# Seven 64x64 block products for eight in the first MLP product of 24 tiles

## The chip, the cores and the metric

The kernel runs on one core of one Trainium2 chip. The metric is the time of one execution on the device, in microseconds (us). Times inside the profile count from the first instruction of one profiled execution; its span ends with the last instruction.

## What is computed

The reference is polysketched attention followed by an MLP with an exact gelu. Cut to what matters (4 batches, 4 heads, 1088 tokens of 32 channels; 4352 tokens of 128 channels in the MLP, 2048 hidden channels):

```python
phi = lambda x: outer(S1 @ x, S2 @ x)          # 8 x 8 = 64 features per token and head
kv, z = sum_s phi(k) v, sum_s phi(k)           # per batch and head
x = (phi(q) @ kv) / (phi(q) @ z + 1e-6)        # -> (4352, 128)
h = x @ w_in                                   # (4352, 2048): the first MLP product
g = 0.5 * h * (1 + erf(h / sqrt(2)))
out = g @ w_out                                # (4352, 128): the second MLP product
```

All of it is in float32.

## The kernel before, in words

**Chunks, tiles, steps.** The tokens are worked in nine chunks n. Chunks 0 to 7 have 512 tokens (two for each batch), chunk 8 has 256, the remainders of all batches. `NMAIN` is 8, `NCH` 2, `NF` 16, `NB` 4. A hidden tile (n, fi) is 128 of the 2048 hidden channels for the tokens of a chunk; four tiles form a block (n, b), stored in one of three `block` buffers. The main loop (L1163) goes over the list `steps` of tiles. The first sixteen steps alternate between chunks 0 and 1; from step 32 on, step t is tile t % 16 of chunk t // 16. So step 64 opens chunk 4 and step 96 chunk 6; step 128 opens chunk 8.

**One step.** `hidden(n, fi)` (L715) multiplies a 128x128 piece of `w_in` with `xT[n]` (128 channels x 512 tokens) into one of two PSUM banks called `h_ps`, as two matmuls of 64 output rows that share the array, and then issues gelu on ACT into the block (L728). After that come `token_sums` if the block is complete, what stands in `slots[t]`, stores in `done[t]` and second products in `products[t]`; drains in `drains[t]` come ahead of the tile. A matmul in the text is two MATMUL instructions in the profile.

**The second product** already uses seven block products for eight. `token_sums` (L764) makes four sums of gelu outputs on POOL (L772 to L775), `channel_sums` has made sums of `w_out`, and `two_products` (L794) multiplies two 128x64 blocks of 256 tokens at a time (L807) into the two `o_ps` banks `acc[n]`. A block has seven such pairs. `drain(n)` (L812) adds the banks up on ACT and DVE into the `sums` tiles, and `store(n)` (L860) finishes with `combine` (L841, L842), a transpose on DVE (L869) and DMAs from SP.

**Where x comes from.** `query_sketch` (L578), `attend_products` (L633) and, for keys, `features_of_all` (L977) use small tiles of the array. `take_x(n)` (L638) copies the attention result of a chunk from `w_ps` banks to `xT[n]` on ACT (L644). For chunks 6, 7 and 8 all this is done in `last_attends` at step 95; chunks 6 and 7 share two `w_ps` banks there.

**Rounding and key work.** At steps 4 to 14 the weights arrive. Key and query transposes (L368, L528) and `query_outer` run on DVE at steps set by `at(t, ...)`.

**What sets the order.** All of it is written out by hand: the lists above give each piece a step, and at the end of the function every instruction is tied to the one before it on its engine, so that each engine works in the order of the text:

```python
    for ins in nc.cur_bb.bb.instructions:
        if ins.engine in last:
            tc.add_manual_dep(ins, last[ins.engine].name, ...)
        last[ins.engine] = ins
```

PSUM has eight banks: two `h_ps`, two `o_ps`, and two `w_ps` tiles of two banks each. A tile's buffer is given on when all that read it are done.

Of the kernel before, what the change touches and what calls it, by code (L numbers as in the profile page):

```python
# [8 lines left out]
FP = mybir.dt.float32  # L9
U32 = mybir.dt.uint32  # L10
AX = mybir.AluOpType
ACT = mybir.ActivationFunctionType
# [4 lines left out]
def kernel(  # L17
# [18 lines left out]
    pe, dve, act, pool, sp = nc.tensor, nc.vector, nc.scalar, nc.gpsimd, nc.sync  # L36
# [5 lines left out]
    NF = d_ff // 128  # L42
# [24 lines left out]
    def work_banks():  # L67

        return wps.tile([128, 2, CW], FP, name="w_ps")
# [645 lines left out]
    def hidden(n, fi, by_halves=False):  # L715
        W = width[n]
        ps = first_banks.pop((n, fi)) if (n, fi) in first_banks else hidden_bank()
        w = w_tile(w_in_sb, fi)
        for rows in (slice(0, 64), slice(64, 128)) if by_halves else (slice(0, 128),):
            if (n, fi) not in begun:  # L720
                pe.matmul(ps[rows, :W], lhsT=w[:, rows], rhs=xT[n][:, :W], start=True, stop=True)  # L721
# [6 lines left out]
        act.activation(out=g_of[n, fi][:, :W], in_=ps[:, :W], func=ACT.Gelu)  # L728
# [61 lines left out]

    def first_block(n):
        return USUAL // NB if n < NCH else 0

    def two_products(n, b, i):  # L794
# [8 lines left out]
        for name, e in zip(two[:2], two[2:]):  # L803
# [3 lines left out]
            pe.matmul(acc[n][bank][half * 64:(half + 1) * 64, col:col + HW], lhsT=fixed, rhs=moving,  # L807
                      start=opens and e == 0 and name in "4715", stop=b == NF // NB - 1, skip_group_check=True)

    drained = {}  # L810

    def drain(n):  # L812


        C, N = (att.tile([128, 2, CW], FP, name="sums") for i in range(2))
        lo, hi, one, two = slice(0, 64), slice(64, 128), slice(0, HW), slice(HW, CW)
        a0, a1 = acc[n]

        act.copy(out=C[lo, 0], in_=a1[hi])
        act.copy(out=N[hi, 0, one], in_=C[lo, 0, one])  # L820

        dve.tensor_copy(out=N[lo, 0, one], in_=a0[lo, one])  # L822
# [4 lines left out]
        dve.tensor_add(out=C[hi, 0, two], in0=a0[hi, two], in1=C[hi, 0, one])  # L827
        dve.tensor_add(out=N[hi, 1, one], in0=a0[hi, one], in1=C[hi, 0, two])
        drained[n] = C, N
# [137 lines left out]
    def at(t, f, *a):  # L967
        slots[t].append(lambda: f(*a))
# [64 lines left out]
    def last_attends():  # L1033

        banks = work_banks()
        attend_products(NMAIN - 2, banks)
        attend_products(NMAIN - 1, banks[:, :, CW // 2:])
        attend_products(NMAIN)
        for n in range(NMAIN - 2, NCHUNK):
            take_x(n)  # L1040

    def turn_keys_rem(pair):
        held["rem"] = work_bank()
# [86 lines left out]
                at(t + 10, turn_first_kv)  # L1130


    products = {t: [] for t in range(len(steps) + LAG)}
    done = {t: [] for t in range(len(steps) + LAG + 1)}
    drains = {t: [] for t in range(len(steps) + LAG + 1)}
    for t, (n, fi) in enumerate(steps):
        if n < NCH and fi < USUAL:
            products[t + LAG].append((project, n, fi))
            if fi == USUAL - 1:
                slots[t + LAG + 1 + 2 * n].append(lambda n=n: take_usual(n))  # L1140
        elif n == NMAIN:
            at_ = max(t + LAG, (n * NF + 5) if fi < 3 else (n * NF + 6) if fi < 5 else 0)
            if fi < NF - 4:
                products[at_].append((project, n, fi))
            if fi == NF - 1:

                products[at_] += [(project, n, NF - f, (i,)) for f, i in ((4, 0), (3, 0), (2, 0), (4, 1), (1, 0), (3, 1),
                                                                          (2, 1), (1, 1))]
                done[at_ + 1].append(n)
        elif fi % NB == NB - 1:  # L1150
            b = fi // NB
            opens = b == first_block(n)
            late = int(n < NCH or n == NCH and opens)
            for later, pairs in ((3, 3), (4, 2), (5, 2)) if opens else ((2, 2), (3, 2), (4, 1), (5, 2)):
                later += late
                for i in range(pairs):
                    products[t + later].append((two_products, n, b, len([p for q in products.values() for p in q
                                                                        if p[:3] == (two_products, n, b)])))
            if b == NF // NB - 1:
                drains[t + 6 + late].append(n)  # L1160
                done[t + 12].append(n)

    for t in range(len(steps) + LAG):  # L1163
        if t < 4:

            hidden(0, t)
            if t == 1:
                w_out[0].low_words()
                w_out[0].exponents()
                w_out[0].finish()  # L1170
                w_out[1].fields()
            if t == 2:
                w_out[1].low_words()
            if t == 3:
                banks = work_banks()
                numerators_by_token(1, halves(banks), range(JC))
                w_out[1].mantissas(by_pool=True)
                w_out[1].exponents()
                divide(1, banks, range(JC), by_head_pair=False)
                w_out[1].signs()  # L1180
                w_out[1].product()
                project(0, 0)
                project(0, 1, cols=slice(0, 256))
                turn_half(1, 0, work_bank(), by_act)
                project(0, 1, cols=slice(256, 512))
                turn_half(1, 1, work_bank(), by_dve)
            continue
        if t == 4:
            first_hidden(1, 0)
            for f, *a in products[t]:  # L1190
                f(*a)
            first_hidden(1, 1)
        for n in drains[t]:
            drain(n)
        sooner = t == NMAIN * NF
        if sooner:
            for f, *a in products[t]:
                f(*a)
        if t < len(steps):
            n, fi = steps[t]  # L1200
            hidden(n, fi, by_halves=t >= 18 and (n < NMAIN or fi < 5))
        if t < len(steps) and steps[t][0] < NMAIN and steps[t][1] % NB == NB - 1:
            n, b = steps[t][0], steps[t][1] // NB
            if b >= first_block(n):
                token_sums(n, b)
        for f in slots[t]:
            f()
        for n in done[t]:
            store(n)
        if t != 4 and not sooner:  # L1210
            for f, *a in products[t]:
                f(*a)
# [41 lines left out]
```

## Time and profile before

| | |
|---|---|
| median of 3 timed runs | 259.19 us (259.15 to 259.4) |
| span of the profiled execution (the page gives no other time of it) | 257.9 us |
| busy: PE, DVE, ACT, POOL | 253.1, 151.1, 115.2, 163.6 us |
| mean granted TensorE clock | 0.999 |
| L721 matmuls (first product), 514 instructions | 136.9 us busy |
| L728 gelu of 512 tokens, 112 instructions | 598 ns each |
| L807 matmuls (second product), 128x64 by 256 tokens | 379 ns each |
| L772 to L775, the sums on POOL | 1278 to 1288 ns each |

PE is TensorE's matmuls, DVE VectorE, ACT ScalarE, POOL GpSimd, SP the engine that issues DMAs. Matmuls overlap one another, so the busy time of single instructions is longer than their share of the stream; the chain of waits gives the share. The chain of waits is followed back from the last instruction and is listed with start, length, and engine and line. In timelines a line gives start, length, engine, line and operation, and in brackets how long the engine had been idle and who released it.

### The profile page before, as it was taken

How to read it: one execution, taken by the hardware profiler on the slowest of the kernel's cores; microseconds unless marked ns; L12 is line 12 of the kernel's file. 1: busy time of each engine (PE TensorE's matmuls, PEld its weight loads, DVE VectorE, ACT ScalarE, POOL GpSimd, SP SyncE). 2: the span in 40 equal slices, each digit the busy share in tenths (PEclk: the TensorE clock that was granted, in tenths of full speed). 3: DMA queues.
4: the chain of work that ended last, by engine and by line, in shares of the span. 5: the costliest groups of instructions: out<-in, count | busy, mean ns of one | idle time of the engine just before them, and what ended most of it. 6: DMA issues, size and time to landing. Idle time of an engine off the chain costs nothing.

```text
span 257.9 us, 5770 instructions
## 1 busy us (share of the span) xinstructions
PE 253.1 (98%) x2335; PEld 135.5 (53%) x2335; DVE 151.1 (59%) x313; ACT 115.2 (45%) x224; POOL 163.6 (63%) x173
## 2 busy tenths in 40 slices
PE   8989999999999999999999999999999999999995
PEld 7846444354444545444444455455544444445794
DVE  3786888969699997590178986399307000700330
ACT  4665777433626332543335332533444334433442
POOL 3313006799968778587758775787758777877300
PEclk9999999999999999999999999999999999999999
DMA  6459747751000101102000002000200200020020
GB/s 203 143 156 375 181 117 174 211 131 15 4 0 13 29 3 23 20 8 35 3 0 3 0 10 37 0 1 3 41 3 5 38 0 1 7 36 0 3 41 20
DMA packets 29594, 13.48 MB, mean 52 GB/s; under 512 B 21888, under 2 KB 27776, under 8 KB 29568
## 3 DMA queue, kind: packets, MB, share of 16 engines
q1 hardware_dynamic: 29392, 13.05, 20.2%
q8 instruction: 18, 0.29, 0.5%
q10 hardware_dynamic: 176, 0.07, 0.1%
q14 instruction: 8, 0.07, 0.1%
HBM read 10.88 MB, written 2.23 MB: 51 GB/s over the span
## 4 chain that ended last, share of the span: by engine, by line
PE 93%; SPq 2%; DMA 2%; DVE 1%; issue 0%; ACT 0%
PE h_ps L721 45%; PE o_ps L807 33%; PE o_ps L858 5%; PE w_ps L855 3%; DMA small<-in_moe_w_in_dram 2%; PE w_ps L437 1%; PE w_ps L578 1%; PE w_ps L633 1%; SPq L132 1%; PE h_ps L737 1%; SPq L100 1%; PE w_ps L977 1%; PE w_ps L656 0%; SPq L118 0%; PE w_ps L467 0%
## 5 line engine op out<-in xcount | busy, mean ns | idle before, releaser
L721 PE MATMUL h_ps<-xT,w_in 128*64 128x512 f32 (+3 forms) x514 | 136.9, 576 | 0.0
L728 ACT ACTIVATE block<-h_ps 128x512 f32<-128x512 f32 (+1 forms) x128 | 73.1, 571 | 117.2 <-PE h_ps L721 115.3
L721 PEld LDWEIGHTS h_ps<-xT,w_in 128*64 128x64 f32 (+1 forms) x514 | 41.9, 142 | 30.5 <-issue 11.6
L807 PE MATMUL o_ps<-block,w_out 128*64 128x256 f32 x224 | 57.5, 379 | 0.0
L772 POOL TENSOR_TENSOR bits_low<-block 128x512 f32<-128x512 f32 x28 | 36.0, 1286 | 27.7 <-ACT block L728 27.7
L807 PEld LDWEIGHTS o_ps<-block,w_out 128*64 128x64 f32 x224 | 30.5, 137 | 38.0 <-issue 27.5
L773 POOL TENSOR_TENSOR bits_a<-block 128x512 f32<-128x512 f32 x28 | 35.8, 1278 | 11.8 <-ACT block L728 11.8
L822 DVE COPY sums<-o_ps 64x256 f32<-64x256 f32 x8 | 3.3, 417 | 60.6 <-PE o_ps L807 60.6
L774 POOL TENSOR_TENSOR bits_e<-bits_a,block 128x512 f32<-128x512 f32 x28 | 36.1, 1288 | 2.2
L775 POOL TENSOR_TENSOR bits_m<-block,bits_e 128x512 f32<-128x512 f32 x28 | 35.9, 1282 | 2.2
L807 PE MATMUL o_ps<-bits_a,small 128*64 128x256 f32 x112 | 28.8, 379 | 0.0
L807 PE MATMUL o_ps<-bits_low,small 128*64 128x256 f32 x112 | 28.8, 379 | 0.0
L807 PE MATMUL o_ps<-block,small 128*64 128x256 f32 x112 | 28.8, 379 | 0.0
L807 PE MATMUL o_ps<-bits_m,w_out 128*64 128x256 f32 x112 | 28.7, 379 | 0.0
L807 PEld LDWEIGHTS o_ps<-block,small 128*64 128x64 f32 x112 | 15.2, 137 | 17.9 <-issue 10.8
L807 PE MATMUL o_ps<-bits_e,small 128*64 128x256 f32 x112 | 17.0, 383 | 0.0
L858 PE MATMUL o_ps<-g,w_out 128*128 128x512 f32 (+1 forms) x34 | 16.5, 572 | 0.0
L807 PEld LDWEIGHTS o_ps<-bits_m,w_out 128*64 128x64 f32 x112 | 15.3, 137 | 0.0
L807 PEld LDWEIGHTS o_ps<-bits_a,small 128*64 128x64 f32 x112 | 15.2, 137 | 0.0
L807 PEld LDWEIGHTS o_ps<-bits_low,small 128*64 128x64 f32 x112 | 15.2, 137 | 0.0
L590 DVE STREAM_TRANSPOSE w_ps<-w_ps 128x512 f32<-128x512 f32 (+1 forms) x7 | 4.8, 687 | 17.1 <-ACT xT L644 12.7
L807 PEld LDWEIGHTS o_ps<-bits_e,small 128*64 128x64 f32 x112 | 7.7, 137 | 10.6 <-issue 8.8
(195 smaller groups left out, 303.7 us busy)
## 6 DMA issues: line engine op xcount, KB each, us to landing
block<-in_moe_w_in_dram SPq DMA_DIRECT2D x3, 512.0 KB, 11.3
block<-in_moe_w_out_dram SPq DMA_DIRECT2D x3, 512.0 KB, 14.7
k<-in_k_dram SPq DMA_DIRECT2D x12, 128.0 KB, 2.9
v<-in_v_dram SPq DMA_DIRECT2D x12, 128.0 KB, 3.5
q<-in_q_dram SPq DMA_DIRECT2D x24, 64.0 KB, 2.1
out_dram<-oT SPq DMA_DIRECT2D x21, 64.0 KB, 2.2
k<-in_k_dram SPq DMA_DIRECT2D x2, 256.0 KB, 2.8
q<-in_q_dram SPq DMA_DIRECT2D x2, 256.0 KB, 3.9
```

Of the source, the lines that this page charges most:

```text
L100: eng.dma_start(out=main[n, b][:, heads], in_=src_of[n][b, heads, 0:MAIN, :].rearrange("h (p j) d -> p h j d", j=J))
L590: dve.transpose(out=tok, in_=ps[:, :, :H2])
L721: pe.matmul(ps[rows, :W], lhsT=w[:, rows], rhs=xT[n][:, :W], start=True, stop=True)
L728: act.activation(out=g_of[n, fi][:, :W], in_=ps[:, :W], func=ACT.Gelu)
L772: pool.tensor_sub(out=s[3], in0=a11, in1=a21)
L773: pool.tensor_add(out=s[1], in0=a21, in1=a22)
L774: pool.tensor_sub(out=s[2], in0=s[1], in1=a11)
L775: pool.tensor_sub(out=s[4], in0=a12, in1=s[2])
L807: pe.matmul(acc[n][bank][half * 64:(half + 1) * 64, col:col + HW], lhsT=fixed, rhs=moving, start=opens and e == 0 and name in "4715", stop ...
L822: dve.tensor_copy(out=N[lo, 0, one], in_=a0[lo, one])
L855: pe.matmul(o_of[n][i][:, :128], lhsT=g[:, i * 128:(i + 1) * 128], rhs=w_tile(w_out_sb, fi), start=first, stop=final)
L858: pe.matmul(o_of[n][:, cols], lhsT=w_tile(w_out_sb, fi), rhs=g[:, cols], start=first, stop=final)
```

## The change

For the blocks (6,2), (6,3) and (7,0) to (7,3), which are 24 of the 128 full tiles, the first product is done in 64x64 blocks. For each pair of tiles, the 2x2 split is over the input channels (upper and lower 64 partitions), the hidden channels (the two tiles) and the tokens (two halves of 256); seven block products stand for eight. It needs sums of `w_in` (`weight_sums`, at steps 57 to 61, kept in tiles of old keys and values), sums of x (`x_sums`, in place of `take_x` for chunks 6 and 7), and copies and additions of partial results (`keep`, `add_to`) before the gelus. Products chain up in one PSUM bank per pair (`chain`), whose partial values are copied out on the way, and in a second bank (`side`).

In the same fourteen slots of such a group (`seven_groups`), the second product of the block two earlier is done in halves of 64 rows, each half into banks of its own (`by_rows`); `keep_rows`, `add_rows` and `drain_rows` bring the two halves together. In each slot two 64x64 tiles work on the lower and two on the upper partitions. The groups stand where step 104 was; steps 104 to 127 do nothing else.

```diff
+    def weight_sums(i):
+        ...
+        ps = work_banks()
+        for to, of in ((LO, HI), (HI, LO)):
+            act.copy(out=ps[to, 0, :n], in_=w_in_sb[i][of])
+        w, o = (t.rearrange("p (q f c) -> p q f c", f=2, c=128) for t in (w_in_sb[i], ps[:, 0, :n]))
+        odd, two = (ps[:, 1, x:x + n // 2].rearrange("p (q c) -> p q c", c=128) for x in (0, HW))
+        act.copy(out=odd, in_=w[:, :, 1])
+        s1, s2, s3, s4 = (t[:, at] for t in WS)
+        dve.tensor_add(out=s1, in0=o[:, :, 1], in1=w[:, :, 1])
+        dve.tensor_sub(out=two, in0=s1, in1=o[:, :, 0])
+        dve.tensor_sub(out=s3, in0=w[:, :, 0], in1=odd)
+        dve.tensor_sub(out=s4, in0=w[:, :, 0], in1=two)
+        act.copy(out=s2, in_=two)
+
+    def x_sums(n):
+        ps = numerators_in[n]
+        take_x(n)
+        ...
+        a, b, pa, pb = xT[n][:, :HW], xT[n][:, HW:], ps[:, 0, :HW], ps[:, 1, :HW]
+        for to, of in ((LO, HI), (HI, LO)):
+            act.copy(out=sb[to], in_=pb[of])
+        dve.tensor_sub(out=t1, in0=pb, in1=a)
+        for to, of in ((LO, HI), (HI, LO)):
+            dve.tensor_sub(out=across[to], in0=pb[of], in1=a[of])
+        dve.tensor_sub(out=t2, in0=pb, in1=across)
+        dve.tensor_sub(out=t4, in0=pa, in1=t2)
+        dve.tensor_sub(out=t3, in0=sb, in1=pb)
+
+    PAIR_AT = {"1": 0, "2": 1, "6": 3, "7": 6, "5": 7, "4": 10, "3": 11}
+    OUT_AT = {0: (1, 2, 4, 8, 9, 10, 11), 64: (0, 4, 5, 6, 7, 12, 13)}
+
+    def pair_product(n, b, k, name):
+        rows, p = (LO, HI)[(k + (name in "2346")) % 2], 2 * b + k
+        for e in range(2):
+            w = w_tile(w_in_sb, 2 * p + (name == "4")) if name in "124" else WS["5673".index(name)][:, p]
+            pe.matmul((chain if name in "1674" else side)[k][e * 64:(e + 1) * 64], lhsT=w[rows, e * 64:(e + 1) * 64],
+                      rhs=XS[n][name][rows], start=name in "125", stop=True, skip_group_check=True)
+
+    def keep(k, i, copy):
+        copy(out=part[k][i], in_=chain[k])
+
+    def add_to(k, to, i):
+        dve.tensor_add(out=results[k][:, to], in0=side[k], in1=part[k][i])
+
+    def after_slot(s, n, b):
+        return {0: [(keep, 0, 0, by_dve)], 1: [(add_to, 0, 0, 0)], 2: [(keep, 1, 0, by_act)],
+                3: [(keep, 0, 1, by_act), (add_to, 1, 0, 0)], 5: [(keep, 1, 1, by_dve)], 6: [(keep, 0, 2, by_dve)],
+                7: [(add_to, 0, 1, 2)], 8: [(keep, 1, 2, by_act)], 9: [(add_to, 1, 1, 2), (pair_gelu, n, b, 0, "both")],
+                10: [(pair_gelu, n, b, 0, "chain")], 11: [(add_to, 0, 2, 1), (pair_gelu, n, b, 1, "both")],
+                12: [(pair_gelu, n, b, 1, "chain")],
+                13: [(add_to, 1, 2, 1), (pair_gelu, n, b, 0, "third"), (pair_gelu, n, b, 1, "third"), (token_sums, n, b)]}.get(s, [])
+
+    def seven_groups(groups, outs, extra):
+        ...
+            for s in range(14):
+                for rows in (LO, HI):
+                    if s in OUT_AT[rows.start]:
+                        row_products(m, mb, OUT_AT[rows.start].index(s), rows)
+                    ...  # pair_product of this slot and these rows
+                for f, *a in after_slot(s, n, b) + extra.get((i, s), []):
+                    f(*a)
...
+        if n == NMAIN - 1:
+            for i in (1, 0):
+                add_rows(i, by_rows[0][i])
...
-        for n in range(NMAIN - 2, NCHUNK):
-            take_x(n)
+        for n in range(NMAIN - 2, NMAIN):
+            x_sums(n)
+        take_x(NMAIN)
...
+    for i, t in ((3, 57), (4, 58), (2, 59), (1, 60), (0, 61)):
+        at(t, weight_sums, i)
+    seven = [(n, b) for n in range(NMAIN - 2, NMAIN) for b in range(NF // NB)]
+    extra = {(3, 5): [(keep_rows, 1)], (3, 8): [(add_rows, 1)], (4, 0): [(keep_rows, 0)], (4, 3): [(add_rows, 0)]}
...
-            at_ = max(t + LAG, (n * NF + 5) if fi < 3 else (n * NF + 6) if fi < 5 else 0)
+            at_ = max(t + LAG, n * NF + (9 if fi < 3 else 10 if fi < 6 else 11 if fi < 9 else 0))
...
+            if n == NMAIN - 2:
+                continue
+            if n == NMAIN - 1:
+                ...  # blocks 2 and 3 of chunk 7 by two_products from steps 128 and 133 on; drain at 137, store at 139
...
-                done[t + 12].append(n)
+                done[t + (12 if n < NMAIN - 3 else 7)].append(n)
...
+            if steps[t] == (NMAIN - 2, 2 * NB):
+                seven_groups(seven[2:], seven[:-2], extra)
+                for i in (1, 0):
+                    keep_rows(i)
+                drain_rows(NMAIN - 2)
+                store(NMAIN - 2)
...
-            hidden(n, fi, by_halves=t >= 18 and (n < NMAIN or fi < 5))
+            hidden(n, fi, by_halves=t >= 18 and (n < NMAIN or fi < 9))
```

`row_products` is `two_products` for one half of the rows, `keep_rows` copies a bank of the upper rows to SBUF on ACT, `add_rows` adds it to the lower rows' bank on DVE, and `drain_rows` is `drain` on those sums. `pair_gelu` is the gelu of two quarters ("both") or of one ("third", "chain").

More of the change, by code (lines that the diff above doesn't have):

```diff
@@ L808, in two_products, with row_products @@
                       start=opens and e == 0 and name in "4715", stop=b == NF // NB - 1, skip_group_check=True)
-    drained = {}
+    LO, HI = slice(0, 64), slice(64, 128)
+    by_rows, begun_rows = {}, set()
+    def row_products(n, b, i, rows):
+        names = (("4", "7"), ("4", "7"), ("6a", "6b"), ("1", "5"), ("1", "5"), ("2", "3"), ("2", "3"))[i]
+        es = ((0, 0), (1, 1), (0, 1), (0, 0), (1, 1), (0, 0), (1, 1))[i]
+        for name, e in zip(names, es):
+            half, bank, col = PLACE[name]
+            moving, fixed = factor(n, b, name, e)
+            first = (n, half, bank, rows.start) not in begun_rows
+            begun_rows.add((n, half, bank, rows.start))
+            pe.matmul(by_rows[rows.start][bank][half * 64:(half + 1) * 64, col:col + HW], lhsT=fixed[rows], rhs=moving[rows],
+                      start=first, stop=False, skip_group_check=True)
@@ new lines @@
+    words_of = lambda t: t.rearrange("p h j d -> p (h j d)")
+    WS, XS = [], {}
+    def weight_sums(i):
+        if not WS:
+            WS.extend(words_of(main[x]).rearrange("p (q c) -> p q c", c=128) for x in (("k", 0), ("v", 0), ("k", 1), ("v", 1)))
+        c0, c1 = pieces[i]
+        n, at = c1 - c0, slice(c0 // 256, c1 // 256)
+        ps = work_banks()
[10 more added lines that the diff above has]
+        act.copy(out=s2, in_=two)
@@ new lines, in x_sums @@
+    def x_sums(n):
+        ps = numerators_in[n]
+        take_x(n)
+        t = words_of(main["kv"[n % 2], 3]).rearrange("p (k x) -> p k x", x=HW)
+        sb, t4 = (mlp.tile([128, CW], FP, name="g", bufs=4)[:, :HW] for i in range(2))
+        t1, across, t2, t3 = (t[:, i] for i in range(4))
+        a, b, pa, pb = xT[n][:, :HW], xT[n][:, HW:], ps[:, 0, :HW], ps[:, 1, :HW]
[7 more added lines that the diff above has]
+        dve.tensor_sub(out=t3, in0=sb, in1=pb)
+        XS[n] = {"1": a, "2": a, "3": b, "4": t4, "5": t1, "6": t2, "7": t3}
@@ new lines @@
+    PAIR_AT = {"1": 0, "2": 1, "6": 3, "7": 6, "5": 7, "4": 10, "3": 11}
+    OUT_AT = {0: (1, 2, 4, 8, 9, 10, 11), 64: (0, 4, 5, 6, 7, 12, 13)}
+    chain, side, part, results = {}, {}, {}, {}
+    def pair_product(n, b, k, name):
[4 more added lines that the diff above has]
+                      rhs=XS[n][name][rows], start=name in "125", stop=True, skip_group_check=True)
@@ new lines, in keep, with pair_gelu @@
+    def keep(k, i, copy):
+        copy(out=part[k][i], in_=chain[k])
+    def add_to(k, to, i):
+        dve.tensor_add(out=results[k][:, to], in0=side[k], in1=part[k][i])
+    def pair_gelu(n, b, k, which):
+        to = blocks[n, b][:, 2 * k:2 * k + 2].rearrange("p f (h x) -> p (f h) x", h=2)
+        r = results[k]
+        out, of = {"both": (to[:, 0::3], r[:, 0:2]), "third": (to[:, 1], r[:, 2]), "chain": (to[:, 2], chain[k])}[which]
+        act.activation(out=out, in_=of, func=ACT.Gelu)
@@ new lines, in seven_groups @@
+    def seven_groups(groups, outs, extra):
+        one, two = [hidden_bank(), hidden_bank()], work_banks()
+        by_rows[64] = halves(work_banks())
+        by_rows[0] = [out_bank(), out_bank()]
+        for k in range(2):
+            chain[k], side[k] = one[k][:, :HW], two[:, k, :HW]
+            results[k] = words_of(main["kv"[k], 2]).rearrange("p (k x) -> p k x", x=HW)
+            part[k] = [words_of(q_sb[4 + k])[:, :HW], words_of(q_sb[4 + k])[:, HW:], words_of(q_sb[6])[:, k * HW:(k + 1) * HW]]
+        for i, ((n, b), (m, mb)) in enumerate(zip(groups, outs)):
+            acc[m] = by_rows[0]
+            blocks[n, b] = block(FP)
+            for f in range(NB):
+                g_of[n, b * NB + f] = blocks[n, b][:, f]
+            for s in range(14):
+                for rows in (LO, HI):
+                    if s in OUT_AT[rows.start]:
+                        row_products(m, mb, OUT_AT[rows.start].index(s), rows)
+                    for k in range(2):
+                        for name, t in PAIR_AT.items():
+                            if t + 2 * k == s and (k + (name in "2346")) % 2 == rows.start // 64:
+                                pair_product(n, b, k, name)
+                for f, *a in after_slot(s, n, b) + extra.get((i, s), []):
+                    f(*a)
@@ new lines, with keep_rows, add_rows, drain_rows @@
+    kept, whole = ([words_of(q_sb[x + i]) for i in range(2)] for x in (0, 2))
+    def keep_rows(i):
+        act.copy(out=kept[i], in_=by_rows[64][i])
+    def add_rows(i, to=None):
+        dve.tensor_add(out=whole[i] if to is None else to, in0=by_rows[0][i], in1=kept[i])
+    drained = {}
+    def drain_rows(n):
+        C, N = (att.tile([128, 2, CW], FP, name="sums") for i in range(2))
+        lo, hi, one, two = LO, HI, slice(0, HW), slice(HW, CW)
+        a0, a1 = whole
+        act.copy(out=C[lo, 0], in_=a1[hi])
+        act.copy(out=N[hi, 0, one], in_=a1[hi, one])
+        dve.tensor_add(out=N[lo, 1, one], in0=a0[lo, two], in1=a0[lo, one])
+        dve.tensor_add(out=C[lo, 1], in0=a1[lo], in1=C[lo, 0])
+        for half in (lo, hi):
+            dve.tensor_add(out=C[half, 0, one], in0=a0[lo, one], in1=C[lo, 1, two])
+        dve.tensor_add(out=C[hi, 0, two], in0=a0[hi, two], in1=C[hi, 0, one])
+        dve.tensor_add(out=N[hi, 1, one], in0=a0[hi, one], in1=C[hi, 0, two])
+        drained[n] = C, N
@@ L1151 @@
             b = fi // NB
+            if n == NMAIN - 2:
+                continue
+            if n == NMAIN - 1:
+                for later, pairs in ((0, 2), (1, 2), (2, 1), (3, 2)) if b > 1 else ():
+                    for i in range(pairs):
+                        products[NMAIN * NF + later + 5 * (b == 3)].append((two_products, n, b, len([
+                            p for q in products.values() for p in q if p[:3] == (two_products, n, b)])))
+                if b == NF // NB - 1:
+                    drains[137].append(n)
+                    done[139].append(n)
+                continue
             opens = b == first_block(n)
@@ L1198 @@
                 f(*a)
+        if t < len(steps) and steps[t][0] in (NMAIN - 2, NMAIN - 1) and (steps[t][0], steps[t][1] // NB) in seven[2:]:
+            if steps[t] == (NMAIN - 2, 2 * NB):
[4 more added lines that the diff above has]
+                store(NMAIN - 2)
+            assert not (slots[t] or products[t] or drains[t] or done[t])
+            continue
         if t < len(steps):
             n, fi = steps[t]
-            hidden(n, fi, by_halves=t >= 18 and (n < NMAIN or fi < 5))
+            hidden(n, fi, by_halves=t >= 18 and (n < NMAIN or fi < 9))
         if t < len(steps) and steps[t][0] < NMAIN and steps[t][1] % NB == NB - 1:
```

## The prediction

> **What bounds the kernel now.** I read the page's busy times first, then the chain of waits, then ACT's and DVE's timelines where the change puts work.
>
> ```profile
> PE 253.1 (98%) x2335; PEld 135.5 (53%) x2335; DVE 151.1 (59%) x313; ACT 115.2 (45%) x224; POOL 163.6 (63%) x173
> PEclk9999999999999999999999999999999999999999
> ```
>
> TensorE is busy throughout at full granted clock, so a shorter stream of products shortens the kernel, and anything that makes PE wait lengthens it one for one. The chain of waits around the steps that get new work:
>
> ```profile
> 119.71 0.43 PE o_ps L807 x4
> 120.15 0.86 PE h_ps L721 x4
> 121.00 0.86 PE o_ps L807 x8
> 121.87 0.86 PE h_ps L721 x4
> ...
> 126.17 0.59 PE w_ps L578 x16
> 126.76 0.43 PE w_ps L633 x16
> 127.19 0.43 PE w_ps L977 x16
> 127.62 0.58 PE o_ps L807 x4
> 128.21 0.86 PE h_ps L721 x4
> ```
>
> A hidden tile (L721) takes 0.86 us, a pair of second-product blocks (x4, L807) 0.43, so a usual step is 1.72. From step 32 on, step t is tile t%16 of chunk t//16: 128.21 is step 64, 120.15 step 60, 115.41 step 57, 184.92 step 96. The L578/L633/L977 bursts show eight 64x32 tiles of the array at work together: 16 instructions of 256 columns in 0.43, the time in which two 128x64 tiles do 4.
>
> ```profile
> 103.19 0.60 ACT L728 ACTIVATE block<-h_ps 128x512 f32<-128x512 f32 x1 [1.04 <-PE h_ps L721]
> 103.68 0.26 ACT L468 COPY kz<-w_ps 128x128 f32<-128x128 f32 x1
> ```
>
> ACT works in the order of the text. A 512-wide operation lasts 0.60, but an independent next one starts 0.49 after it; a 256-wide one lasts 0.39 (next after 0.29). ACT's gelu of a tile must end before PE writes the tile two steps later (two h_ps banks).
>
> ```profile
> 193.15 0.42 DVE L822 COPY sums<-o_ps 64x256 f32<-64x256 f32 x1 [10.22 <-PE o_ps L807]
> ...
> 195.41 0.43 DVE L827 TENSOR_TENSOR sums<-o_ps,sums 64x256 f32<-64x256 f32 x1
> 195.88 0.43 DVE L828 TENSOR_TENSOR sums<-o_ps,sums 64x256 f32<-64x256 f32 x1
> 196.34 0.82 DVE L841 TENSOR_TENSOR sums<-sums 64x256 f32<-64x256 f32 x1
> 197.17 0.42 DVE L842 TENSOR_TENSOR sums<-sums 64x256 f32<-64x256 f32 x1
> 197.63 0.71 DVE L869 STREAM_TRANSPOSE oT<-sums 128x512 f32<-128x512 f32 x1
> ```
>
> A DVE operation of 256 columns with a PSUM operand takes 0.41 to 0.43, a dependent one starts 0.46 after it, an independent one about 0.36. DVE is in chunk 5's drain and store until 198.34.
>
> **The seven-product groups: -2.58.** A block of four tiles now costs PE 4 x 0.86 + 7 x 0.43 = 6.45. In a group it is 28 + 28 quarter products (64x64, 256 columns), four at a time: 14 slots of 0.43 = 6.02. Six groups save 6 x 0.43 = 2.58. That a slot takes 0.43 with four tiles is taken from L633 and L977 (eight tiles, 0.43). Entering a 64-row mode costs 0.16 (L578's 0.59 against 0.43), leaving it 0.15 (L807 x4 in 0.58): +0.31, bounds 0.15 and 0.31.
>
> Inside a group the chain bank must be copied out (`keep`) two slots (0.86) before it is written again. Data are readable 0.22 after the product gives way to the next (tile 58's gelu starts at 118.04, the product behind tile 58 at 117.82), the copy takes 0.41, PE restarts 0.10 after a release (xT's copy ends 184.65, the product starts 184.75): 0.73 against 0.86, no stall. By kinder and harsher hand-overs 0 to 0.14 per tight slot, with `add_rows` about 2 in all; I take 0, and keep 2 for the range. ACT has about 3.9 of 6.02 to do (3 copies and 4 gelus of 0.39, 2 gelus of 0.60), DVE nine operations of 0.41 = 3.7, POOL its four sums of 1.28 plus gaps = 5.3: each fits. The Trainium skill, "TensorEngine Tiling (Array Packing)", PSUM Bottleneck, speaks against the change: tiling speeds TensorE but not the emptying of PSUM, which may become the bound. By that rule a group would last as long as its busiest emptier, 3.9 by the rows above, so it would not bind here.
>
> **First group's first copy: +1.9.** Steps 101 to 103 lose their products (moved into the groups), so they run at 0.86 each from 193.10, and the groups begin at 195.7 on the chain. The copy of `chain[0]` after slot 0 stands on DVE behind chunk 5's drain and store (whose end, 198.34, does not move). It would be ready at 196.3, starts at 198.3, ends at 198.7; slot 3, due at about 196.95 by PE's own row, starts at 198.85. Everything behind it on PE waits 1.9. Bounds 1.4 (if L841 takes 0.42) and 2.1.
>
> **weight_sums at steps 57 to 61: +6.0.** For a 512-wide piece, with the step's gelu starting at G, ACT issues copies at G+0.49 and +0.98 (ends +1.56) and `odd` at +1.47. DVE: s1 at +1.61, `two` at +2.07 (ends +2.48), s3 +2.43, s4 +2.84 (ends +3.25). ACT's last copy, s2, reads `two`; the next gelu is queued behind it. Two bounds: s2 starts when `two` is there (+2.53; next gelu +2.82), or, as s3 and s4 read the same PSUM bank and stand ahead in the text, when s4 is done (+3.30; next gelu +3.59). The trace has ACT and DVE on one bank at the same time nowhere that I looked: in the drain DVE's L823 (193.60) starts after ACT's read of that bank (L819, 192.99 to 193.57), while L822, on the other bank, runs beside it. L823 also needs L819's result, so this is no proof; I take the later start, nearest to that row. The Trainium skill, "PSUM — Partial Sum Buffer", PSUM bank collisions raise a hardware error, says that two engines may not touch one bank and quadrant at once, reads included, so that a program must order them; by it W is 6.0, without it 3.7. No run here shows it yet.
>
> With 3.59 for 512-wide pieces and, likewise, 2.65 for the two 256-wide ones (128-wide operations 0.26 to 0.29), gelus start at 116.32 (step 57), 119.91, 123.50, 127.09, 129.74, 132.39 (step 62). PE restarts on the chain 0.27 after a release (184.65 to 184.92). Tile 60, due at 120.15, needs gelu 58 (ends 120.51): 120.78. Tile 61 needs gelu 59: 124.37. Tile 62: 127.96. Tile 63: 130.61. Gelu 63 starts at 132.88, chunk 4's `take_x` runs 133.37 to 133.96, tile 64 starts at 134.23 instead of 128.21: +6.0. Chunk 2's store (1.5 of DVE) and key transposes (1.26) now stand behind these sums and mostly fit. With 2.82 the same walk gives +3.7. Over both readings and quicker or slower hand-overs: 2.2 to 8.5. ACT's copies alone, without the way over DVE, would give 0.
>
> **x_sums at step 95: +1.5.** `take_x(6)` 184.06 to 184.65 stays, so tile 96 starts as now. Behind it on ACT: two 64x256 copies (end 185.23), then `take_x(7)`, which reads the same two banks as chunk 6's six DVE operations. If ordered behind them (185.28 to 187.6), ACT goes on 187.65, 188.14, 188.43, `take_x(8)` 188.72, and tile 96's gelu runs 189.0 to 189.6 instead of from 185.91; tile 98, due 188.37, starts 189.87: +1.5. If banks may be shared, that gelu starts at 186.5 and the cost is 0. The same choice as above; bounds 0 and 1.8. The rest of DVE's work ends before the drain of 193.15, now 1.5 later too.
>
> **After the groups: +0.5.** ACT has the last gelus (about 1.0 past the end), two `keep_rows` and two copies of `drain_rows` before tile 128's gelu, which ends about 3.1 past; tile 130, due at 2.7, starts at 3.2. Bounds 0 and 0.9. Chunk 6's drain and store and chunk 7's later one (5.6 of DVE, 2.6 of SP issue) end before PE does: after chunk 7's last product PE still has 7 x 0.43 + 64 x 0.11 = 10.1. POOL's last sums end 6.4 past the groups, needed at 8.6.
>
> **The other edits, nothing.** The new times of chunk 7's and chunk 8's products and `by_halves` up to tile 8 change the order of PE's work, not its amount; chunk 5's store, five steps earlier in the text, already runs right after its drain (196.34), so DVE and SP see no change; `drain`'s two `add_rows` (0.68 each) lie in the 10.1 that PE still has.
>
> **Sum.** -2.58 + 0.31 + 1.9 + 6.0 + 1.5 + 0.5 = +7.6. The span would go from 257.9 to 265.5. The page gives the profiled execution no time but its span; the timed median, 259.19, lies 1.29 above it, and nothing at either end changes: 266.8 us.
>
> **Rivals.** (a) ACT and DVE may read one bank together: 3.7 for 6.0 and 0 for 1.5, +3.8: 263.0. For it: nothing in the rows forbids it. Against: the drain's order. (b) Faster: ACT's sums fit its idle time. Place: steps 57 to 63 (and 95); ACT has 1.23 idle per step, the copies take 1.56 for three steps and 1.02 for two. If the way over DVE costs ACT nothing, W and x_sums are 0, the sum is +0.1, and with the low ends elsewhere (1.4, 0.15, 0) -1.0: 258.2. It decides from W below 0.5. Against: s2 stands ahead of the next gelu and needs two dependent DVE results. (c) The hand-overs in the groups are too long for two slots: +2 more, 268.8. (d) Four quarter tiles do not run at 0.43: each 0.01 per slot costs 0.84 over 84 slots; at 0.50, 272.7. Against: L633, L977.
>
> **Numbers.** Forecast 0.63, its own range 264.5 to 269; (a) 0.11; (b) 0.12; (c) 0.10; (d) 0.04. The range, 260.3 to 270.5, leaves out most of (b), (d) and the harsh end of weight_sums. A measurement of this kernel can tell about 0.2% (0.5 us) from no change. Faster: most of (b) and no other, 0.09; within 0.2%: the rest of (b) and the kindest end of (a), 0.04; slower 0.87.
>
> **What would show it.** In the chain after: tiles 60 to 64 late by 6 in all, PE idle before L721 released by ACT's gelu; ACT's s2 copies starting after s4. A gap of 1.9 at slot 3 of the first group released by DVE; then slots of 0.43, groups of 6.02. I am wrong if ACT keeps pace in steps 57 to 63 (then near 259), or if a slot is not 0.43.

## The result

The changed kernel takes **286.03 us** (median of 4 runs, 285.02 to 286.83); the kernel before, run beside it, 259.26 (4 runs, 259.15 to 259.4). The ratio is 1.1027 (95% interval 1.0999 to 1.1056): 26.8 us slower, where +7.6 was forecast and the range ended at 270.5. The profiled execution took 285.02 us with a span of 283.2, which is 25.3 above the span before; the steps below are laid against that. The times measured for the runs below are medians, and a run over 1.5% longer than the fastest of its kernel is left out (there is one, 277.52 us, of `e4_sides_apart`).

The busy times and the clock row of the changed kernel's page:

```profile
PE 265.0 (94%) x2751; PEld 143.3 (51%) x2751; DVE 191.8 (68%) x402; ACT 134.3 (47%) x282; POOL 164.0 (58%) x173
PEclk9999999999999999989999999999988999999999
```

PE was busy 98% of a span of 257.9 and is now busy 94% of one of 283.2. The clock row, flat in the kernel before, has two dips, each at or just behind a place where PE waited for over 2 us.

The chain of waits of the changed kernel at steps 57 to 64 (start, length, engine and line):

```profile
114.99 0.88 PE h_ps L721 x4
115.90 0.60 ACT block L728
116.52 0.59 ACT w_ps L836
117.14 0.59 ACT w_ps L836
117.75 0.39 ACT w_ps L839
118.16 0.44 DVE k L841
118.62 0.44 DVE w_ps L842
...
119.42 0.42 DVE v L844
119.87 0.37 ACT v L845
120.24 0.50 ACT block L728
...
136.48 1.08 PE h_ps L721 x4
```

Before, this stretch of the chain was PE alone. Now it goes through ACT (L836 the two copies, L839 `odd`, L845 s2) and DVE (L841 to L844, s1, `two`, s3, s4), and returns to a gelu (L728); in ACT's timeline the first four of these gelus start at 115.90, 120.14, 124.46 and 128.70, 4.24 to 4.32 us apart. Step 57's tile starts at 114.99 (before: 115.41) and step 64's at 136.48 (before: 128.21): `weight_sums` costs 0.42 + 8.27 = 8.7.

The first group, DVE's timeline of the changed kernel (start, length, engine, line, operation, idle time before and its releaser):

```profile
206.55 0.43 DVE L968 TENSOR_TENSOR sums<-o_ps,sums 64x256 f32<-64x256 f32 x1
206.99 0.83 DVE L981 TENSOR_TENSOR sums<-sums 64x256 f32<-64x256 f32 x1
207.83 1.39 DVE L982 TENSOR_TENSOR sums<-sums 64x256 f32<-64x256 f32 x1
209.26 0.71 DVE L1009 STREAM_TRANSPOSE oT<-sums 128x512 f32<-128x512 f32 x1
210.00 0.42 DVE L878 COPY q<-h_ps 128x256 f32<-128x256 f32 x1
210.53 0.42 DVE L881 TENSOR_TENSOR k<-w_ps,q 128x256 f32<-128x256 f32 x1
```

The group begins on PE at 206.37; its first copy (`keep`, L878) and first addition (`add_to`, L881) stand behind chunk 5's drain and store. That is as forecast, except that PE waits for the addition too, as its timeline has it:

```profile
211.01 0.69 PE L874 MATMUL w_ps<-xT,w_in 64*64 64x256 f32 x2 [3.12 <-DVE k L881]
```

The group lasts to 218.40, 12.03 instead of 7.9.

A later group, DVE's timeline and then PE's (only its products into `w_ps`, the tile of the two `side` banks; two rows are the four MATMULs of one side product):

```profile
231.96 0.42 DVE L881 TENSOR_TENSOR v<-w_ps,q 128x256 f32<-128x256 f32 x1 [0.82 <-ACT block L888]
233.13 0.42 DVE L881 TENSOR_TENSOR k<-w_ps,q 128x256 f32<-128x256 f32 x1 [0.75 <-PE h_ps L874]
234.31 0.42 DVE L881 TENSOR_TENSOR v<-w_ps,q 128x256 f32<-128x256 f32 x1 [0.75 <-PE w_ps L822]
...
235.49 0.42 DVE L881 TENSOR_TENSOR k<-w_ps,q 128x256 f32<-128x256 f32 x1 [0.25 <-PE w_ps L874]
```

```profile
232.44 0.43 PE L874 MATMUL w_ps<-xT,v 64*64 64x256 f32 x2 [0.15 <-DVE v L881]
232.71 0.38 PE L874 MATMUL w_ps<-xT,v 64*64 64x256 f32 x2
233.62 0.43 PE L874 MATMUL w_ps<-xT,v 64*64 64x256 f32 x2
233.88 0.38 PE L874 MATMUL w_ps<-xT,v 64*64 64x256 f32 x2
234.79 0.43 PE L874 MATMUL w_ps<-xT,w_in 64*64 64x256 f32 x2
...
235.97 0.43 PE L874 MATMUL w_ps<-xT,w_in 64*64 64x256 f32 x2
```

The two pairs' side products alternate, k into one bank, v into the other. Each begins 0.06 or 0.07 after the addition that reads the *other* bank has ended (232.38, 233.55, 234.73, 235.91): 1.17 or 1.18 from one to the next, where two slots are 0.86. PE's row at 232.44 names an addition on DVE as what released it.

At step 95, in `x_sums`, the chain runs from chunk 6's last DVE operation (L862) over `take_x(7)` (L644) to tile 96's gelu and tile 98:

```profile
196.16 0.34 DVE k L862
...
196.52 0.05 ACT xT L644
...
198.28 0.49 ACT block L728
...
198.82 1.08 PE h_ps L721 x4
```

POOL's first sum of each group gives the period (its timeline, L772 alone):

```profile
219.57 1.27 POOL L772 TENSOR_TENSOR bits_low<-block 128x512 f32<-128x512 f32 x1 [7.87 <-ACT block L888]
227.42 1.27 POOL L772 TENSOR_TENSOR bits_low<-block 128x512 f32<-128x512 f32 x1 [2.65 <-ACT block L888]
235.27 1.27 POOL L772 TENSOR_TENSOR bits_low<-block 128x512 f32<-128x512 f32 x1 [2.64 <-ACT block L888]
243.60 1.27 POOL L772 TENSOR_TENSOR bits_low<-block 128x512 f32<-128x512 f32 x1 [3.12 <-ACT block L888]
251.79 1.27 POOL L772 TENSOR_TENSOR bits_low<-block 128x512 f32<-128x512 f32 x1 [2.99 <-ACT block L888]
259.64 1.28 POOL L772 TENSOR_TENSOR bits_low<-block 128x512 f32<-128x512 f32 x1 [2.63 <-ACT block L888]
```

Five periods of 7.85, 7.85, 8.33, 8.19 and 7.85, together 40.07; the same work took 5 x 6.45 = 32.25 before, and 5 x 6.02 = 30.1 was forecast.

All the steps of the span: -0.42 up to step 57, +8.7 `weight_sums`, +0.2 to step 95, +1.95 `x_sums`, +0.4 to the groups, +5.6 the first group (12.03 - 6.45), +7.8 the other five, +1.1 after them (24.6 from the groups' end instead of 23.5). Sum: +25.3.

### The profile page after: what moved, and what is told of

Its sections match the earlier page's. It is cut to its first block, busy times and chain, and to the rows that moved or that the text cites. A ratio compares the mean times of both kernels' runs of the same rounds, so it can differ in the third digit from the quotient of the medians.

```text
span 283.2 us, 6810 instructions
## 1 busy us (share of the span) xinstructions
PE 265.0 (94%) x2751; PEld 143.3 (51%) x2751; DVE 191.8 (68%) x402; ACT 134.3 (47%) x282; POOL 164.0 (58%) x173
## 4 chain that ended last, share of the span: by engine, by line
PE 76%; DVE 9%; ACT 7%; POOL 4%; issue 2%; DVEq 0%; POOLq 0%; ACTq 0%
PE h_ps L721 31%; PE o_ps L807 21%; PE o_ps L998 5%; PE w_ps L874 4%; PE w_ps L995 3%; ACT block L728 2%; DVE k L881 2%; ACT w_ps L836 2%; PE h_ps L874 1%; DVE v L881 1%; ACT block L888 1%; POOL bits_e L774 1%; POOL bits_low L772 1%; PE w_ps L437 1%; POOL bits_a L773 1%
## 5 line engine op out<-in xcount | busy, mean ns | idle before, releaser
L721 PE MATMUL h_ps<-xT,w_in 128*64 128x512 f32 (+3 forms) x426 | 113.4, 575 | 8.0 <-ACT block L728 7.8
L728 ACT ACTIVATE block<-h_ps 128x512 f32<-128x512 f32 (+1 forms) x104 | 58.5, 566 | 84.5 <-PE h_ps L721 81.1
L772 POOL TENSOR_TENSOR bits_low<-block 128x512 f32<-128x512 f32 x28 | 36.0, 1285 | 54.1 <-ACT block L728 32.1
L721 PEld LDWEIGHTS h_ps<-xT,w_in 128*64 128x64 f32 (+1 forms) x426 | 34.2, 143 | 38.3 <-ACT block L728 13.7
L807 PE MATMUL o_ps<-block,w_out 128*64 128x256 f32 x176 | 45.2, 379 | 0.0
L807 PEld LDWEIGHTS o_ps<-block,w_out 128*64 128x64 f32 x176 | 24.0, 137 | 29.0 <-issue 20.7
L807 PE MATMUL o_ps<-block,small 128*64 128x256 f32 x88 | 23.5, 391 | 0.0
L807 PE MATMUL o_ps<-bits_low,small 128*64 128x256 f32 x88 | 23.5, 391 | 0.0
L881 DVE TENSOR_TENSOR v<-w_ps,q 128x256 f32<-128x256 f32 x18 | 7.6, 425 | 14.3 <-PE h_ps L874 5.4
L878 ACT COPY q<-h_ps 128x256 f32<-128x256 f32 x18 | 6.7, 373 | 21.7 <-PE h_ps L874 21.7
L822 PE MATMUL w_ps<-block,w_out 64*64 64x256 f32 x48 | 13.7, 386 | 0.3 <-ACT q L927 0.3
L728 ACT ACTIVATE g<-h_ps 128x512 f32<-128x512 f32 x16 | 9.5, 595 | 7.0 <-PE h_ps L721 4.8
L962 DVE COPY sums<-o_ps 64x256 f32<-64x256 f32 x7 | 2.9, 417 | 14.6 <-PE o_ps L807 14.6
L881 DVE TENSOR_TENSOR k<-w_ps,q 128x256 f32<-128x256 f32 x18 | 7.6, 425 | 6.9 <-PE h_ps L874 4.5
```

The lines of the kernel that those rows point to most:

```text
L772: pool.tensor_sub(out=s[3], in0=a11, in1=a21)
L822: pe.matmul(by_rows[rows.start][bank][half * 64:(half + 1) * 64, col:col + HW], lhsT=fixed[rows], rhs=moving[rows], start=first, stop=Fals ...
L881: dve.tensor_add(out=results[k][:, to], in0=side[k], in1=part[k][i])
```

## The experiments

Theory A at the start: the whole loss is three separate things, the weight sums, the x sums and the groups, and the groups lose because the two side banks lie in one tile. The rivals: the slots themselves are slow, or the copies out of the chain bank are too long.

### One part at a time

`e1_weight_sums_alone` is the kernel before with `weight_sums` at its five steps, and nothing that reads the sums; `e2_x_sums_alone` is the kernel before with `x_sums` at step 95; `e3_groups_alone` is the changed kernel without either. In short:

```diff
 # e1: the kernel before, with
+    for i, t in ((3, 57), (4, 58), (2, 59), (1, 60), (0, 61)):
+        at(t, weight_sums, i)
 # e2: the kernel before, with
-        for n in range(NMAIN - 2, NCHUNK):
-            take_x(n)
+        for n in range(NMAIN - 2, NMAIN):
+            x_sums(n)
+        take_x(NMAIN)
 # e3: the changed kernel, with
-            x_sums(n)
+            take_x(n)
+            a, b = xT[n][:, :HW], xT[n][:, HW:]
+            XS[n] = {"1": a, "2": a, "3": b, "4": a, "5": b, "6": a, "7": b}
-        at(t, weight_sums, i)      # WS points at keys and values
```

> The kernel before, with weight_sums at steps 57 to 61 and nothing else of the change; the sums are made and not read. Theory A (ACT is held in each of these steps by its own copies, one after the other, and by the way over DVE, and PE waits for the gelus): about 8.7 us above before, 268, as the chain of the changed kernel is 8.7 longer from step 57 to step 64. Theory B (the loss in those steps comes from something else of the change, such as a slower clock or moved work): less than 6 us above.

Measured: 269.1 (268.86 to 269.85), ratio 1.0382 (1.0358 to 1.0406): **+9.8**, theory A and 1.1 dearer.

> The kernel before, with x_sums in place of take_x for chunks 6 and 7; the sums are made and not read. Theory A (chunk 7's take_x waits behind chunk 6's sums on DVE, and tile 96's gelu behind it): 1.9 us above before, 261.2, as in the changed kernel's chain between the attention products of step 95 and tile 98. Theory B (its cost there came from the lateness of the steps before): 0 to 0.5.

Measured: 261.65, ratio 1.0083 (1.0066 to 1.0100): **+2.3**, theory A.

> The changed kernel without weight_sums and with plain take_x: its block products read keys, values and x in place of the sums, so the time alone is meant. Theory A (the groups themselves lose time, since products into one side bank wait for the addition that reads the other): 16 us above before, about 275, groups of 7.85 us except the first, which has DVE's drain and store of chunk 5 in front. Theory B (the groups are slow because the steps before them disturbed their order or the clock): close to before, 256.5 to 260.

Measured: 273.89, ratio 1.0551 (1.0509 to 1.0593): **+14.6**, theory A. POOL's period is that of the changed kernel (7.84, 7.84, 8.33, 7.84, 7.84).

The three add up to 26.7, the whole loss of 26.8. So the parts add up, and each can be looked into by itself. More than half of the loss is in the groups, where a gain was forecast.

### The side banks in tiles of their own

`e4_sides_apart` changes which tile each bank belongs to: the two side banks become the two one-bank `o_ps` tiles, and the lower rows' banks of the second product, which are read once per chunk, share a `w_ps` tile; chunk 8's output takes one `o_ps` bank for one of its two work banks. `keep_rows` and `add_rows` move by three slots or fewer. The products, copies and additions are the same.

```diff
-        one, two = [hidden_bank(), hidden_bank()], work_banks()
+        one, two = [hidden_bank(), hidden_bank()], [out_bank(), out_bank()][::-1]
-        by_rows[0] = [out_bank(), out_bank()]
+        by_rows[0] = halves(work_banks())
-            chain[k], side[k] = one[k][:, :HW], two[:, k, :HW]
+            chain[k], side[k] = one[k][:, :HW], two[k][:, :HW]
```

> The changed kernel with the two side banks in PSUM tiles of their own (they take the o_ps banks; the lower rows' banks go into a w_ps tile, and keep_rows and add_rows move to slots where the row halves are not being written). Theory A (products into one side bank wait for the addition that reads the other bank of the same tile): groups 1 to 5 take 6.0 to 6.3 us for 7.85 to 8.3, the first about 2 less too, 11 to 12 us below the changed kernel, 274 to 275. Theory C (the hand-over of the chain bank within two slots is what is too long): groups stay at 7.5 or more, less than 2 us below. Theory D (64x64 tiles run slower than 0.43 a slot): no change.

Measured: 272.31 (272.11 to 272.76), ratio 1.0499 (1.0478 to 1.0520): 13.7 less than the changed kernel, where theory A had 11 to 12. POOL's timeline, L772 alone:

```profile
216.45 1.28 POOL L772 TENSOR_TENSOR bits_low<-block 128x512 f32<-128x512 f32 x1 [4.57 <-ACT block L888]
222.54 1.27 POOL L772 TENSOR_TENSOR bits_low<-block 128x512 f32<-128x512 f32 x1 [0.87 <-ACT block L888]
228.59 1.28 POOL L772 TENSOR_TENSOR bits_low<-block 128x512 f32<-128x512 f32 x1 [0.82 <-ACT block L888]
```

The period is 6.03 to 6.22 over all five, against 6.02 forecast. So the slots run at 0.43 with four 64x64 tiles, and the chain banks' copies fit: it was the tile that two banks shared. The first group, from its first product to that of the next, takes 8.76 (206.52 to 215.28) instead of 12.03.

`e8_groups_alone_sides_apart` is e3 with that edit, to see what is left of the groups.

> The groups alone (block products that read keys, values and x in place of the sums, so the time alone is meant), with the side banks in tiles of their own. Theory A: with 0.43 a slot and no cross wait, -2.58 + 0.3, DVE's drain in front of the first group 1.9, the end of the groups 0.6, small waits 0.5: 259.5 to 260.5. Theory B (the groups lose more elsewhere): above 262.

Measured: 261.91 (260.79 to 262.87, 10 runs), ratio 1.0082 (1.0056 to 1.0108): +2.4. That lies between the two theories, 1.4 above the upper end of A. PE's timeline of this run shows one long stall in the groups, in the first:

```profile
199.23 0.43 PE L874 MATMUL h_ps<-xT,v 64*64 64x256 f32 x2 [2.19 <-DVE q L878]
```

It is the stall of the prediction (1.9), here 2.19: with the sides apart PE waits for `keep` behind the store, and no longer for `add_to` behind `keep`.

### The sums without ACT

`e6_sums_by_dma_alone` puts the weight sums alone on the kernel before (`x_sums` is not called), but the halves of `w_in` change places by DMAs from SP, and DVE makes the sums from SBUF alone; ACT does nothing for the weight sums.

```diff
+    def swap_halves(i):
+        ...
+        for to, of in ((LO, HI), (HI, LO)):
+            sp.dma_start(out=to_tile[to], in_=w_in_sb[i][of])
 ...
-        dve.tensor_sub(out=two, in0=s1, in1=o[:, :, 0])
-        dve.tensor_sub(out=s3, in0=w[:, :, 0], in1=odd)
-        dve.tensor_sub(out=s4, in0=w[:, :, 0], in1=two)
-        act.copy(out=s2, in_=two)
+        dve.tensor_sub(out=s3, in0=w[:, :, 0], in1=w[:, :, 1])
+        dve.tensor_sub(out=s2, in0=s1, in1=o[:, :, 0])
+        dve.tensor_sub(out=s4, in0=w[:, :, 0], in1=s2)
```

> The kernel before, with the sums of w_in made by DMA (the swapped halves) and DVE (from SBUF alone), and not read; nothing else. Theory A (the 9.8 us of weight_sums are ACT's): within 0.3 us of before. Theory B (the DVE work itself, ahead of the store of chunk 2 and the key transposes, or its traffic beside POOL, costs time): 1 us or more above.

Measured: 262.19, ratio 1.0095 (1.0061 to 1.0128): +2.6, theory B. Without ACT, 7.2 of the 9.8 us are gone; the work on DVE has a price of its own. The list of waits from 115 to 135 us (who waited for whom: us in total, times, longest):

```profile
PEld w_ps L1021 <- DVE kT L368: 2.7, 2, 2.3
PE w_ps L1021 <- DVE kT L368: 1.8, 1, 1.8
```

The key transposes (L368) of step 61 stand behind the sums in DVE's order and end at 128.71; PE's features of the keys (L1021) wait for them, and step 64 starts at 130.56 instead of 128.21. This run was 0.22 ahead of the kernel before at 109 us, in front of the sums (chunk 2's drain on DVE starts at 108.78 instead of 109.00), so the sums cost 2.57 here: the whole loss. The DVE operations take up to 1.50 each, where others of their kind take 0.41 to 0.42 in the same trace.

`e7_s2_by_dve_alone` is e1 with one copy moved, s2 from ACT to DVE, so that the next gelu no longer waits for DVE.

```diff
-        act.copy(out=s2, in_=two)
+        dve.tensor_copy(out=s2, in_=two)
```

> weight_sums alone on the kernel before, as it was measured at 9.8 us above, but with its last copy (s2 from two) on DVE, so that ACT keeps its three copies and never waits for DVE. Theory A (most of the loss is the way over DVE in front of the next gelu): ACT has 2.4 us to do in three steps of 1.72 and under 1.72 in two, less 1.9 of room: 0.3 to 2 us above before. Theory B (the copies themselves are the loss, since each waits for the one before): 5 us or more.

Measured: 264.81 (262.94 to 266.13), ratio 1.0174 (1.0108 to 1.0240): +5.2. By the medians the way over DVE is 4.6 of e1's 9.8. But the four runs lie in two pairs: 262.94 and 263.6 with a mean granted clock of 1.0, which is 3.4 to 4.0 above before and between the two theories, and 266.03 and 266.13 with 0.987. Of what is left the profile, taken of the run of 266.13, shows three causes and not the shares of the first two. ACT's timeline:

```profile
116.27 0.60 ACT L728 ACTIVATE block<-h_ps 128x512 f32<-128x512 f32 x1 [1.06 <-PE h_ps L721]
116.89 1.20 ACT L822 COPY w_ps<-w_in 64x512 f32<-64x512 f32 x2
118.12 0.38 ACT L825 COPY w_ps<-w_in 128x256 f32<-128x256 f32 x1
118.43 0.59 ACT L728 ACTIVATE block<-h_ps 128x512 f32<-128x512 f32 x1
```

The three copies into one `w_ps` tile start 0.61 and 0.62 apart, each after the end of the one before, not 0.49 apart: a step with sums takes ACT 2.16, and PE 1.72. And DVE, which has all the rest and the key transposes between, ends the last piece at 130.38; PE's features of the keys follow at 130.51. Third, from 129.8 to 136.6 the granted clock is 0.5, and PE is busy for 6.08 of these 6.8 us; the two pairs of runs differ by 2.4 to 3.2.

### All mended

`e5_all_mended` is the changed kernel with the sides apart, the sums as in e6, `x_sums` with all three `take_x` first and its copies between two halves on ACT at steps 97 and 98, the first group's three DVE copies on ACT, chunk 6's `drain_rows` and `store` at step 128 and chunk 7's `keep_rows` at steps 130 and 131.

```diff
+        by_dve = act.copy if (n, b) == (NMAIN - 2, 2) else dve.tensor_copy
 ...
+            at(n + 91, x_swap, n)
 ...
+    at(NMAIN * NF, drain_rows, NMAIN - 2)
+    at(NMAIN * NF, store, NMAIN - 2)
+    for i in (1, 0):
+        at(NMAIN * NF + 3 - i, keep_rows, i)
```

> The changed kernel with every loss that the traces name taken away: the side banks in tiles of their own; the swapped halves of w_in by DMA, and its sums on DVE from SBUF alone; all three take_x ahead of x's sums, the swapped x copied by ACT at steps 97 and 98; the first group's chain copies all on ACT, so that they need not wait for DVE's drain of chunk 5; keep_rows and drain_rows of chunk 6 at steps 128 to 131 behind the gelus. Theory A (these five were all of the loss): 2.58 saved, 0.3 for the two mode switches, some 0.5 left in the groups: 256.8 to 258.0, faster than before. Theory B (something is left, such as the two-slot hand-over of the chain or the 64x64 mode): 259 or more.

Measured: 261.26 (260.86 to 261.46, 11 runs), before 259.56 (22 runs), ratio 1.0062 (1.0042 to 1.0081). The time lies 3.3 above the upper end of theory A. In the chain the features wait for the key transposes as in e6: step 64's tile starts at 130.15, and step 95's products (L633) at 184.88 instead of 182.93. This run was 0.63 ahead in front of the sums (108.37 for 109.00), so it is 2.57 again, as in e6.

Two runs tell apart where those 2.6 us are to be had. `e9_sums_later` is e5 with the weight sums behind the key transposes; `e10_groups_mended` is e5 without the sums.

```diff
-    for i, t in ((3, 57), (4, 58), (2, 59), (1, 60), (0, 61)):
-        at(t - 7, swap_halves, i)
+    for i, t in ((3, 62), (4, 62), (2, 62), (1, 84), (0, 84)):
+        at(55, swap_halves, i)
         at(t, weight_sums, i)
```

> The mended version (sides in tiles of their own, halves of w_in swapped by DMA, first group's copies on ScalarE) with one more edit: the weight sums stand behind the key transposes in VectorE's order (three of five at step 62, in the 12.35 us in which VectorE waits in the kernel before, two at step 84). Theory A, the loss that is left in the mended version is the key transposes that end 128.7 us into the run behind the sums: TensorE's features then start as before (step 64 at 128.2 to 128.6 instead of 129.57), and the time is the mended version's 261.3 less 1.4 to 2.0, 259.3 to 259.9. Theory B, the sums' VectorE operations cost what they cost wherever they stand, since beside GpSimd they take up to 1.49 us instead of 0.42: the query features of step 64 come late instead, step 64 to 68 is 1 us late or more, and the time stays at 260.8 to 261.5.

Measured: **258.67** (258.17 to 259.27, 12 runs), before 259.45 (23 runs), ratio 0.9971 (0.9960 to 0.9983): 0.8 us faster than the kernel before, with the reference's whole computation, and 2.6 faster than e5. DVE's timeline of e9:

```profile
113.72 1.26 DVE L368 STREAM_TRANSPOSE kT<-k 128x512 f32<-128x512 f32 x2
114.91 0.97 DVE L844 TENSOR_TENSOR k<-v,w_in 128x256 f32<-128x256 f32 x1
115.81 1.49 DVE L845 TENSOR_TENSOR k<-w_in 128x256 f32<-128x256 f32 x1
117.22 0.41 DVE L846 TENSOR_TENSOR v<-k,v 128x256 f32<-128x256 f32 x1
...
124.80 1.37 DVE L847 TENSOR_TENSOR v<-w_in,v 128x256 f32<-128x256 f32 x1
127.33 0.73 DVE L590 STREAM_TRANSPOSE w_ps<-w_ps 128x512 f32<-128x512 f32 x1 [1.16 <-ACT xT L644]
```

The sums are as slow as in e5 (up to 1.50), but now nobody waits: three of the five pieces fill the idle 12.35 us in front of L590 and leave 1.16 of it. Step 64's tile starts at 127.62, 0.59 ahead of before; the run was 0.59 ahead already at 110 us (109.81 for 110.40 in chunk 2's drain), so the step stands where it did. Theory A holds: the time is 0.6 below its lower end.

> Time only: the block products read keys, values and x itself instead of their sums, so no weight sums and no x sums are made. Otherwise the mended version: sides in tiles of their own, the first group's copies on ScalarE, and the drain of the row sums of the chunk before at its own steps. Theory A, what groups with sides apart still lose (261.9 against 259.6) is the 2.19 us in which TensorE waits in the first group for VectorE's copy behind the drain: without it 259.3 to 259.9. Theory B, the loss is at the end of the groups (the copies, additions and gelu between the last group and tile 130) and stays: 261 or more.

Measured: 258.43 (258.23 to 259.45, 12 runs), ratio 0.9963 (0.9951 to 0.9974). Theory A again, lower by 0.9 than its lower end. PE waits 0.89 in the first group instead of e8's 2.19, and from the start of the last group's sums on POOL to the end of the span it takes 22.9 instead of e8's 23.6, which is part of the loss that theory B named. e9 is 0.24 above e10, and their intervals overlap: placed as in e9, all the sums together cost next to nothing.

## Why the prediction was wrong

- **"Inside a group ... no stall": the step that failed.** The hand-over itself was right: 0.73 was forecast from the end of a product's slot to the next product, and 1.17 - 0.43 = 0.74 is measured. It was laid against the chain bank, which has two slots for it, and not against the side banks, where the two pairs' products leave one slot (0.43) in between if the tile is one. I had counted banks; in this program the order is kept by tile, and `two[:, 0]` and `two[:, 1]` are one. A group has five such intervals. In the second group of the changed kernel they take 1.18, 1.29, 1.24, 1.18 and 1.18, together 1.77 more than ten slots of 0.43, of the 1.83 by which 7.85 exceeds 6.02. The "about 2" kept for the range was for six groups; it was 10 for five. Shown by e4: other tiles, the same work, 6.03 to 6.22. The diff had what was needed: `one, two = [hidden_bank(), hidden_bank()], work_banks()` gives `one` two tiles and `two` a single one.
- **Groups, -2.58 and rival (d).** Right once the tile is mended: e10 gains 1.0 after a stall of 0.89 and what is left at the ends. Rival (d) is refuted: slots run at 0.43. Rival (c) had the right place with a size of 2; by its mechanism (two slots too short for the chain bank's copies) it is wrong.
- **First group, +1.9.** The mechanism was right; 2.19 with sides apart (e8), 3.12 as changed, because the addition behind the copy gates PE too. The group as a whole was 4.1 longer than the forecast 7.9. With the sides apart it takes 8.76 (e8 and e4); with the shared tile and a granted clock of 1.0, in e3, 10.63 (195.48 to 206.11) with nearly the same wait, 3.14; in the changed kernel 12.03, with a granted clock of 0.5 from 210.5 to 213.9, where PE's products stand 0.42 apart instead of 0.21. So the 4.1 are 0.86 for the copy's wait and what goes with it, 1.87 for the shared tile and 1.40 for the clock, which the forecast did not have.
- **`weight_sums`, +6.0.** Right mechanism and right choice between its two readings: the gelu waits for s2, and s2 for s4. The size was off: 8.7 in the span, 9.8 alone. A 512-wide piece takes 4.24 to 4.32 instead of 3.59: by the rows the copies stand end to end (0.62 apart, not 0.49), and s1 starts 0.03 after the end of `odd`, which lies in the tile's other bank and isn't read by s1: s1 at +2.26 after the gelu instead of +1.61. That looks like the same error as in the groups; no run takes it apart. The three wide pieces are 2.0 longer in all and the two narrow ones (3.08 and 3.07 for 2.65) 0.85, together 2.9, where the forecast and the span differ by 2.7.
- **`x_sums`, +1.5.** 1.95 in the span (above the bound of 1.8), 2.3 alone. The order was as forecast: ACT's `take_x(7)` waits for chunk 6's last DVE operation on the shared banks.
- **Rivals (a) and (b)** fell with `weight_sums`. Whether ACT and DVE may read one bank together was not tried: in every run here the program orders them. The Trainium skill, "PSUM — Partial Sum Buffer", PSUM bank collisions raise a hardware error, stood behind the dearer reading, and the measured order agrees: s2 starts 0.04 after the end of s4, at 119.87. But it speaks of bank and quadrant, and what cost most here was an order between two different banks.
- **Other edits nothing, and after the groups +0.5.** 0.2 + 0.4 between the parts and +1.1 after the groups, slightly dearer than forecast.

Where it came out: 9.8 + 2.3 + 14.6 are 26.7 of the 26.8. With the order mended, the arithmetic that is saved brings 0.8 us (e9).

## What to carry to other kernels

Count tiles, not banks, when you ask what a write waits for: two banks of one tile that two streams use in turn are one buffer, and their hand-overs add up in the faster stream. Price each hand-over from the product's end through the copy to the next product, and lay it against the slots between two uses of the *tile*. Side work that an engine off the critical path has room for is free only in the right place of that engine's order: look for the idle stretch in its timeline and put the work behind whatever the critical engine needs next.

## What the runs showed of the hardware

- **Granted clock.** In the kernel before it is 1.0 but for the last half microsecond. In the changed kernel it is also 0.5 for 3.41 us twice, at 125.2 to 128.6 and 210.5 to 213.9. Both times PE had waited much just before, for ACT or DVE: of the 3.41 us ahead it was busy for 1.04 and 0.78. In the first, a tile takes 1.95 instead of 1.03 in PE's timeline:

```profile
125.11 1.95 PE L721 MATMUL h_ps<-xT,w_in 128*64 128x512 f32 x4 [2.37 <-ACT block L728]
```

  The Trainium skill, "TensorE: Matmul & The Clock Gate", What's actually happening, tells of a free-running window of about 3.4 us, after an idle one of which the clock is halved; the lengths measured here agree, though PE was not idle for the whole of the 3.41 us ahead. The second stretch is 1.4 of the loss (e3's first group against the changed kernel's). In the first the chain runs through ACT and DVE, so that PE's slower tile is not on it.
- **DVE beside POOL.** A DVE addition of 256 columns with both operands in SBUF takes 0.41 to 0.42, or more, up to 1.50, while POOL has its sums (1.27 to 1.46 each). In e9, L845 starts at 115.81 and lasts 1.49; POOL's sum runs from 115.68 to 117.01, and L845 ends 0.29 after it. The Trainium skill, "SBUF — State Buffer", Terms, describes a port pair that DVE and GpSimd hold for a whole instruction; these rows agree. Additions of 256 columns that read a PSUM operand took 0.41 to 0.43 in all the stretches shown here.
- **Four 64x64 tiles** in float32 do a slot of 256 columns in 0.43, the same as two 128x64 and eight 64x32 ones.
